# A mixer product in seven 64-row halves per tile instead of eight, in a three-stage block on one Trainium2 core

## The chip, the core and the metric

The kernel runs on one core of a Trainium2 chip. The core has a matrix engine (PE, whose weight loads are listed as PEld), three elementwise engines (DVE, ACT, POOL) and a queue, SP, from which this kernel issues all its DMAs. Time is device time of one execution in microseconds, lower is better. Before the change the median of three runs is 190.23 us (189.8 to 190.86).

## What is computed

The input x has 2048 rows of 448 bf16 numbers. With LN for layer normalisation without weights:

```
h   = x + Attention(LN(x))          16 heads of 28; each row attends to rows i, i-2, ..., i-14
n   = LN(h)
y   = gelu(LN(n) @ w1)              448 -> 448
g0..g3 = four groups of 112 columns of y, moved by +1, -1, +2, -2 rows, zeros moved in
n1  = n + concat(g0, g1, g2, g3) @ w2
out = h + n1 + gelu(LN(n1) @ w3) @ w4       448 -> 1792 -> 448
```

The change concerns `y` (the mixer's first product and its gelu) and the product with `w2` (the mixer's second product).

## The kernel before, in words

Rows are handled in four blocks of 512 rows (t = 0 to 3) up to the mixer's first product, and in five units after it (2, 4, 4, 4 and 2 tiles of 128 rows). The phases of a block are N1 (first normalisation), A1 (queries, keys), V (values), A2 (products of queries and shifted keys), S (softmax), A3 (weighted values), O (output product and residual), B1 (second normalisation) and M (the mixer's first product with its gelu). The phases of a unit are B2 (the mixer's second product), T (third normalisation), W3 (448 -> 1792 with gelu) and B3 (1792 -> 448 and the store). A block or unit number follows the name: M1 is the first product of block 1, B21 the second product of unit 1.

**Matmuls in pairs of halves.** Most products have a contraction of 448, cut into pieces of at most 64 rows. Two pieces run at once, one in the upper and one in the lower 64 rows of the array. `duo` takes two output groups A and B and lists their upper and lower pieces: in a first series A's upper pieces run beside B's lower ones, in a second B's upper beside A's lower. Seven pieces of 64 rows would hold 448 exactly, and the products over normalised rows do it so: their transposed copies overlap by 64 rows, so that one output of a pair takes four upper and three lower pieces and the other three and four (`sums`).

**The mixer's second product** can't do so before the change, because its contraction is split by the row shifts: each group of 112 lies in `gT` in partitions 0 to 111, and is read at its own shift (`SHIFT`). A tile takes an upper piece of 64 and a lower piece of 48 rows from each of four groups, that is eight pieces, and a pair of tiles 16 matmuls of 448 columns. There are eight such pairs of tiles in the kernel (one in B20, two each in B21, B22, B23, one in B24).

**The order of the work** is a table of numbers, `ORDER`: operation k of the recorded program stands at the place that the table gives it, and each engine and the SP queue carry out their operations in the order in which they stand there. Waits are then derived from what each operation reads and writes, and from eight PSUM banks and small pools of buffers that are given out along the table. `OTHER` names operations that run on their second engine: copies out of PSUM that DVE makes instead of ACT, and residual additions that DVE makes instead of POOL. An engine waits at the head of its list, and all behind it waits too.

**ACT's tables.** `gelu` and the `exp`/`ln` of the softmax and of the normalisations need different tables on ACT. Each change from one to the other is an ACT_TABLE_LOAD; there are 12 in the program, before and after.

All instructions of the engines are issued from one line (L1012 before, L1032 after), so the profile's groups are told apart by the names of the tiles: `w_s,arena` are the mixer's second product, `actT,w_s` its first, `arena<-ps 112x512` its gelus, `xin<-ps` the attention's residual, `wo_s,actT` its output product, `qk_r` the products of A2, `bd_r` the spread weights of A3, `h3T<-ps` the gelus of W3, `lntm` normalised rows.

Of the kernel before, what the change touches and what calls it, by code (L numbers as in the profile page):

```python
# [5 lines left out]
ACT = mybir.ActivationFunctionType  # L6
# [13 lines left out]
STAGE = '....'  # L20
ALONE = False
ORDER = """
# [29 lines left out]
"""  # L52
OTHER = """
94 187 189 549 550 551 685 686 755 756 815 816
"""
FULL = (4,)
FILL = (1, 1, 0, 0)
# [228 lines left out]
def bass_sequential_preLN__sliding_local_dilated__mixer_s_mlp__prompt_kernel(  # L286
# [6 lines left out]
    NST = SEQ // 512  # L293
# [11 lines left out]

    SHIFT = (-1, 1, -2, 2)
    GC = D // 4


    A_W3 = 0  # L310
# [9 lines left out]
    with ExitStack() as es:  # L320
        def sb(name, shape, dt):
            return es.enter_context(nc.sbuf_tensor(name, shape, dt))
# [8 lines left out]
        actT = sb("actT", [128, NACT, 4, 4, 128], BF16)  # L331
        h3T = sb("h3T", [128, NF + 2, 512], BF16)
        wo_s = sb("wo_s", [128, 4, D], BF16)
        w1_s = sb("w1_s", [128, 4, D], BF16)
        w2_s = sb("w2_s", [128, 4, D], BF16)
        ident = sb("ident", [128, 128], BF16)
        zc = sb("zc", [128, 4, 2, 32], BF16)
# [115 lines left out]
        wo_v = A_wo.rearrange("(c j k) n -> j k c n", c=4, j=4)  # L453
        for j in range(4):
            dma("wo%d" % j, wo_s[32 * j:32 * j + DH, :, :], wo_v[j], DH * D * 8)
        load_rows("w1", w1_s, B_w1, 0, D)
        dma("w2", w2_s[0:GC, :, :], B_w2.rearrange("(c k) n -> k c n", k=GC), D * D * 2)
        load_rows("w3", w3_s, B_w3, 0, F)
        loads = [op for op in S.ops if op.is_dma]
        for a, b in zip(loads, loads[1:]):  # L460
            b.odeps.add(a)
# [390 lines left out]
        def phase_B1(t):  # L852
            ln = _Tile(P_ln)
            summed = STATS["B1"][t] == "a"
            if summed:
                sums_stats(1, range(4 * t, 4 * t + 4), lambda i: xin[:, i, :], ln)
            else:
                for i in range(4 * t, 4 * t + 4):
                    ln_stats(1, xin[:, i, :], i)
            norms = norms_of("B1", t, 4)  # L860
            rstd(1, 4 * t, 4, summed, norms, POWER["B1"][t])
            for n, i in enumerate(range(4 * t, 4 * t + 4)):
                normalize(1, i, ln, n, xin[:, i, :], TURN["B1"][t], summed, norms[n])
            a = transposed(ln, TURN["B1"][t])
            S.tag = "M%d" % t

            def group(g, upper):
                b = _Tile(P_bank)
                return sums(lambda lo, n: b(halves(lambda v: v[0:GC, lo:lo + n], n // 128)), lambda c, part: w1_s[part, c, g * GC:(g + 1) * GC],
                            lambda c, part, lo, n: rows(a, c, lo // 128, n // 128, part), upper), \  # L870
                    lambda: act(gT[0:GC, g, 2 + t * 512:2 + (t + 1) * 512], b(lambda v: v[0:GC, :]), ACT.Gelu_apprx_tanh)

            for g in (0, 2):
                (A, ev_a), (B, ev_b) = group(g, True), group(g + 1, False)
                duo(A, B, ((0, 512),))
                ev_a()
                ev_b()
# [10 lines left out]
        def phase_B2(u):  # L888
            tiles = UNITS[u]
            summed = STATS["B2"][u] == "a"  # L890

            def group(i):
                b = _Tile(P_bank)

                def side(part):
                    return [(gT[part, c, 2 + i * 128 + SHIFT[c]:130 + i * 128 + SHIFT[c]], (lambda lo, m, c=c: w2_s[part, c, lo:lo + m])) for c in range(4)]

                def out():
                    kw = dict(accum_out=mv[:, 2, i, 0:1]) if summed else {}
                    dve("scalar_tensor_tensor", out=xb[i], in0=xin[:, i, :], scalar=rs_y[:, 1, 0, i:i + 1], in1=b(lambda v: v[:, 0:D]), op0=ALU.mult, op1=ALU.add, **kw)  # L900
                    if not summed:
                        ln_stats(2, xb[i], i)

                return (lambda lo, n: b(lambda v: v[:, lo:lo + n]), side(TOP), side(slice(64, GC))), out

            for i in tiles[::2]:
                (A, out_a), (B, out_b) = group(i), group(i + 1)
                duo(A, B, ((0, D),))
                out_a()
                out_b()  # L910
            ln = _Tile(P_ln)
            if summed:
                sums_stats(2, tiles, lambda i: xb[i], ln)
            S.tag = "T%d" % u
            norms = norms_of("B2", u, len(tiles))
            rstd(2, tiles[0], len(tiles), summed, norms, POWER["B2"][u])
            for n, i in enumerate(tiles):
                normalize(2, i, ln, n, xb[i], TURN["B2"][u], summed, norms[n])
            for i in tiles:
                both = dict(out=xb[i], in0=xb[i], in1=xin[:, i, :], op=ALU.add)  # L920
                S.add("pool", "tensor_tensor", alts=[("dve", [("tensor_tensor", both)])], **both)
            b2_a[u] = transposed(ln, TURN["B2"][u], len(tiles))
# [131 lines left out]
```

## Time and profile before

| | before |
|---|---|
| median of 3 runs | 190.23 us (189.8 to 190.86) |
| the profiled execution | 188.86 us, its span 187.1 us |
| PE busy | 179.9 us, 96% of the span |
| DVE busy | 129.1 us, 69% |
| ACT busy | 124.6 us, 67% |
| POOL busy | 19.8 us, 11% |
| granted TensorE clock | 1.0 |

A row of the chain of waits gives its start, its length and the work; a row of the timeline its start, its length, engine, line, operation, output and inputs, shapes, the count of merged instructions, and in brackets the idle time just ahead and who ended it. A table by stretches gives for each stretch the busy time of each engine with the count of its instructions. A matmul's own duration is its latency; two halves of the array and successive matmuls overlap, so the pace of matmuls is read from the distance of starts.

### The profile page before, as it was taken

Reading aid. Unit: us, or ns where it says so; the run is one execution under the profiler, and the core shown is the slowest. Engines: PE = TensorE matmul, PEld = TensorE weight load, DVE = VectorE, ACT = ScalarE, POOL = GpSimd, SP = SyncE. Lnnn points to the kernel's source line nnn. Section 1 sums busy time; section 2 is a strip of 40 time slices with the busy share of each in tenths; the row PEclk is TensorE's granted clock in tenths of the full one; section 3 lists DMA queues with packets and bytes.
Section 4 is the critical chain, followed back from the end, with each engine's and each line's share of the span. In section 5 each row is a group of like instructions: output and inputs, shape, how many; then the busy total and the mean of one; then the engine's idle time right before and its main releaser. Section 6 shows DMA issues by size and latency. Waiting matters only on the chain.

```text
span 187.1 us, 5625 instructions
## 1 busy us (share of the span) xinstructions
PE 179.9 (96%) x2434; PEld 96.1 (51%) x2434; DVE 129.1 (69%) x233; ACT 124.6 (67%) x286; POOL 19.8 (11%) x50
## 2 busy tenths in 40 slices
PE   6899999989989989999999999999999999999994
PEld 2586434345433555565655455555555444455773
DVE  6899999999999999999797930196871015005222
ACT  3579999999999999999674977910275013830340
POOL 3430000000000002000240000037045000000000
DMA  5924193356307996596543060016005004300012
GB/s 146 346 101 104 12 188 69 77 126 143 105 4 117 213 257 263 88 332 116 126 31 85 5 137 0 4 22 157 10 0 116 0 0 129 77 0 28 0 53 75
DMA packets 36576, 18.05 MB, mean 96 GB/s; under 512 B 25304, under 2 KB 36040, under 8 KB 36552
## 3 DMA queue, kind: packets, MB, share of 16 engines
q1 hardware_dynamic: 36552, 17.70, 39.5%
q8 instruction: 19, 0.31, 0.7%
q14 instruction: 5, 0.04, 0.1%
HBM read 7.91 MB, written 1.84 MB: 52 GB/s over the span
## 4 chain that ended last, share of the span: by engine, by line
PE 78%; DVE 16%; ACT 3%; DMA 1%; issue 1%
PE ps L1012 78%; DVE bd_r L1012 7%; DVE qk_r L1012 4%; DVE lntm L1012 2%; DVE st L1012 1%; DMA xin<-in_A_x_dram 1%; DVE mx L1012 1%; DVE ls L1012 1%; ACT vt L1012 1%; ACT xin L1012 0%; ACT ls L1012 0%; DVE pb L1012 0%; ACT arena L1012 0%; ACT rs_x L1012 0%; ACT rs_y L1012 0%
## 5 line engine op out<-in xcount | busy, mean ns | idle before, releaser
L1012 PE MATMUL ps<-actT,arena 64*128 64x512 bf16 (+1 forms) x756 | 69.6, 329 | 0.2
L1012 ACT ACTIVATE h3T<-ps 128x512 bf16<-128x512 f32 (+1 forms) x70 | 30.9, 518 | 41.1 <-PE ps L1012 40.8
L1012 PEld LDWEIGHTS ps<-actT,arena 64*128 64x128 bf16 x756 | 37.0, 94 | 28.0 <-PE ps L1012 1.9
L1012 PE MATMUL ps<-arena,h3T 64*128 64x448 bf16 (+2 forms) x434 | 45.4, 343 | 0.1
L1012 DVE SCALAR_TENSOR_TENSOR ost<-ps,mrs,arena 128x448 bf16<-128x448 f32 (+1 forms) x17 | 10.7, 653 | 37.4 <-PE ps L1012 33.7
L1012 ACT ACTIVATE arena<-ps 128x512 bf16<-128x512 f32 (+3 forms) x64 | 32.3, 542 | 6.2 <-PE ps L1012 5.8
L1012 PEld LDWEIGHTS ps<-arena,h3T 64*128 64x128 bf16 (+1 forms) x434 | 23.6, 94 | 18.9 <-PE ps L1012 0.5
L1012 DVE TENSOR_TENSOR qk_r<-arena 128x4096 bf16<-128x4096 bf16 (+1 forms) x16 | 32.0, 2014 | 0.1
L1012 POOL TENSOR_TENSOR arena<-arena,xin 128x448 f32<-128x448 f32 x9 | 10.9, 1243 | 96.6 <-DVE lntm L1012 96.6
L1012 DVE TENSOR_TENSOR bd_r<-arena,bmask 80x2048 bf16<-80x2048 bf16 x16 | 18.8, 1215 | 0.2
L1012 DVE TENSOR_SCALAR lntm<-arena,mv,rs_y 128x512 bf16<-128x512 f32 x14 | 7.2, 537 | 13.2 <-ACT rs_y L1012 11.4
L1012 PE MATMUL ps<-wo_s,actT 64*128 64x448 bf16 x128 | 14.5, 350 | 0.8 <-ACT actT L1012 0.6
L1012 PE MATMUL ps<-w_s,arena 64*128 64x448 bf16 (+1 forms) x128 | 14.5, 350 | 0.1
L1012 ACT ACTIVATE actT<-ps 128x512 bf16<-128x512 f32 (+2 forms) x21 | 12.8, 648 | 1.5 <-PE ps L1012 1.5
L1012 PE MATMUL ps<-actT,w_s 64*112 64x512 bf16 x112 | 13.4, 378 | 0.1
L1012 PE MATMUL ps<-arena,actT 64*128 64x448 bf16 x112 | 13.1, 349 | 0.1
L1012 ACT ACTIVATE lntm<-xin,nm 128x448 bf16<-128x448 bf16 x16 | 10.5, 662 | 2.6 <-DVE nm L1012 2.4
L1012 DVE SCALAR_TENSOR_TENSOR arena<-xin,rs_y,ps 128x448 f32<-128x448 bf16 x16 | 10.4, 672 | 0.4 <-PE ps L1012 0.4
L1012 PEld LDWEIGHTS ps<-actT,w_s 64*112 64x112 bf16 x112 | 7.0, 127 | 4.8 <-PE ps L1012 0.5
L1012 DVE BATCH_NORM_STATS2 st<-xin 128x6 f32<-128x448 bf16 x16 | 9.1, 613 | 0.4 <-DMA xin<-in_A_x_dram 0.4
L1012 PEld LDWEIGHTS ps<-wo_s,actT 64*128 64x128 bf16 x128 | 5.5, 94 | 6.8 <-ACT actT L1012 1.5
L1012 PEld LDWEIGHTS ps<-w_s,arena 64*128 64x128 bf16 (+1 forms) x128 | 6.0, 94 | 5.8 <-PE ps L1012 0.5
(69 smaller groups left out, 155.1 us busy)
## 6 DMA issues: line engine op xcount, KB each, us to landing
arena<-in_B_w_dram SPq DMA_DIRECT2D x2, 896.0 KB, 6.4
out_dram<-ost SPq DMA_DIRECT2D x15, 112.0 KB, 2.3
arena<-in_B_w_dram SPq DMA_DIRECT2D x2, 784.0 KB, 6.1
vw<-vt SPq DMA_DIRECT2D x4, 320.0 KB, 3.9
vw<-vt SPq DMA_DIRECT2D x4, 256.0 KB, 4.3
arena<-in_A_wqkv_dram SPq DMA_DIRECT2D x2, 448.0 KB, 4.5
xin<-in_A_x_dram SPq DMA_DIRECT2D x2, 448.0 KB, 5.0
xin<-in_A_x_dram SPq DMA_DIRECT2D x3, 224.0 KB, 5.0
```

The lines of the kernel that those rows point to most:

```text
L1012: inst = getattr(eng, meth)(**kw)
```

## The change

Group 3's 112 columns of `y` are split: 64 of them (336 to 399) stay a group of their own, and the other 48 (400 to 447) are dealt out, 16 to each of the groups 0, 1 and 2, which so become 128 rows high. The first product computes the 16 columns together with a group's own 112 (`w1_s` now holds 128 columns per group, put together by six loads and two copies on POOL), and computes group 3's 64 columns twice, in the upper and the lower half. The 16 rows belong to another shift than the group they ride in. So each of the groups 0 to 2 gets, besides its gelu of 128x512, a second gelu of the 16 rows from the same PSUM bank, written 3, 1 or 4 columns further left, over what the first gelu left there. In the last block three small memsets fill what is moved in. In the second product a tile then takes seven pieces of 64 rows: four upper and three lower for the first tile of a pair, three and four for the second. `w2_s` holds the rows in the same arrangement (four loads instead of one).

```diff
+    GX = 16
-        w1_s = sb("w1_s", [128, 4, D], BF16)
+        w1_s = sb("w1_s", [128, 4, 448 + 112], BF16)
...
-        load_rows("w1", w1_s, B_w1, 0, D)
-        dma("w2", w2_s[0:GC, :, :], B_w2.rearrange("(c k) n -> k c n", k=GC), D * D * 2)
+        for c in range(4):
+            dma("w1%s" % "abcd"[c], w1_s[:, c, 0:384].rearrange("p (g n) -> p g n", g=3)[:, :, GX:],
+                B_w1[64 * (0, 2, 3, 5)[c]:64 * (0, 2, 3, 5)[c] + 128, 0:3 * GC].rearrange("k (g n) -> k g n", g=3), 128 * 3 * GC * 2)
+        load_rows("w1e", w1_s[:, :, 448:448 + GC], B_w1, 3 * GC, GC)
+        dma("w2", w2_s[GX:128, 0:3, :], B_w2[0:3 * GC, :].rearrange("(c k) n -> k c n", k=GC), 3 * GC * D * 2)
+        dma("w2x", w2_s[0:GX, 0:3, :], B_w2[400:, :].rearrange("(c k) n -> k c n", k=GX), 3 * GX * D * 2)
+        for h in range(2):
+            dma("w2%s" % "ab"[h], w2_s[64 * h:64 * h + 64, 3, :], B_w2[3 * GC:400, :], 64 * D * 2)
         load_rows("w3", w3_s, B_w3, 0, F)
+        pool("tensor_copy", out=w1_s[:, :, 0:384].rearrange("p c (g n) -> p c g n", g=3)[:, :, :, 0:GX], in_=w1_s[:, :, 512:].rearrange("p c (g n) -> p c g n", g=3))
+        pool("tensor_copy", out=w1_s[:, :, 384:448], in_=w1_s[:, :, 448:512])
...
-                    lambda: act(gT[0:GC, g, 2 + t * 512:2 + (t + 1) * 512], b(lambda v: v[0:GC, :]), ACT.Gelu_apprx_tanh)
+                def evict():
+                    at = 2 + t * 512
+                    act(gT[:, g, at:at + 512], b(), ACT.Gelu_apprx_tanh)
+                    if g < 3:
+                        at -= SHIFT[3] - SHIFT[g]
+                        skip = max(0, -at)
+                        act(gT[0:GX, g, at + skip:at + 512], b(lambda v: v[0:GX, skip:]), ACT.Gelu_apprx_tanh)
+                        if t == NST - 1:
+                            pool("memset", ap=gT[0:GX, g, at + 512:2 + SEQ], constant=0.0)
...
-                return (lambda lo, n: b(lambda v: v[:, lo:lo + n]), side(TOP), side(slice(64, GC))), out
+                return (lambda lo, n: b(lambda v: v[:, lo:lo + n]), side(TOP, 3 + upper), side(BOT, 4 - upper)), out
...
 ORDER = """
-29 0 1 6 7 33 34 35 5 8 48 9 53 49 39 40 41 42 43 44 45 46 47 30 32 2 50 54 11 10 58 51 52 60 59 55 61 56 62 57 63 65
...
+5 38 39 0 1 48 49 50 51 52 53 54 55 56 42 45 7 6 8 40 57 58 9 62 63 2 59 60 61 11 10 67 69 68 70 64 65 71 72 66 73 96
...
 OTHER = """
-94 187 189 549 550 551 685 686 755 756 815 816
+103 117 195 197 402 516 522 573 574 636 637 638 639 707 778 779 781 840
```

The table of numbers is a new one for the whole program, and three kinds of work changed engine with it: four copies out of PSUM went from ACT to DVE (one in A10, one in A32, two in A33), and two of the residual additions from POOL to DVE. Two places of the order matter to the prediction.

ACT from the end of the softmax of block 2 to the first gelus of W30. `arena<-ps 80x512` are the softmax's last copies, then come the gelus of M0, copies of A32 (`actT<-ps`) and A13 (`arena<-ps 128x512`), the statistics of B20 (`lntm,mv<-arena,nm`), the gelus of M1, and the statistics of block 2 (`lntm,mv<-xin,nm`). Before:

```order
L1012 ACTIVATE arena<-ps 80x512 x2
L1012 ACT_TABLE_LOAD
L1012 ACTIVATE arena<-ps 112x512 x4
L1012 ACTIVATE actT<-ps 128x512 x3
L1012 ACTIVATE arena<-ps 128x512 x2
L1012 ACTIVATE actT<-ps 128x512
L1007 ACT_TABLE_LOAD
L1012 ACTIVATE rs_y<-rs_x 128x4
L1012 ACTIVATE lntm,mv<-arena,nm 128x448 x2
L1012 ACTIVATE rs_x<-mv,epsilon 128x2
L1012 ACTIVATE rs_y<-rs_x 128x2
L1012 ACT_TABLE_LOAD
```

And of the change, from the gelus of M0 (the three rows with 16 partitions and the two of 128x512 around them) on:

```order
L1032 ACTIVATE arena<-ps 16x510
L1032 ACTIVATE actT<-ps 128x512
L1032 ACTIVATE arena<-ps 128x512
L1032 ACTIVATE actT<-ps 128x512
L1032 ACTIVATE arena<-ps 128x512
L1027 ACT_TABLE_LOAD
L1032 ACTIVATE rs_y<-rs_x 128x4
L1032 ACTIVATE lntm,mv<-arena,nm 128x448 x2
L1032 ACTIVATE rs_x<-mv,epsilon 128x2
L1032 ACTIVATE actT<-ps 128x512
L1032 ACTIVATE rs_y<-rs_x 128x2
L1032 ACT_TABLE_LOAD
```

Seven gelus of M0 stand where four stood, four copies instead of six ahead of the table load, and one copy of A32 has moved behind it, between the `ln` and the `exp` of T0; after the last load come seven gelus of M1 instead of four.

PE from the first product of block 0 to the second product of unit 1. `actT,w_s` are M0 and M1, `bd_r,vw` A32, `wo_s,actT` O2, `qk_r,zc` A23, `w_s,arena` B20 and then B21, `actT,arena 128x256` W30. Before:

```order
L1012 MATMUL ps<-actT,w_s 112x512 x28
L1012 MATMUL ps<-bd_r,vw 32x64 x96
L1012 MATMUL ps<-w_s,arena 128x448 x8
L1012 MATMUL ps<-bd_r,vw 32x64 x32
L1012 MATMUL ps<-w_s,arena 128x448 x8
L1012 MATMUL ps<-wo_s,actT 128x448 x8
...
L1012 MATMUL ps<-actT,w_s 112x512 x14
L1012 MATMUL ps<-qk_r,zc 32x32x8x2 x16
L1012 MATMUL ps<-w_s,arena 128x448 x16
L1012 MATMUL ps<-actT,arena 128x256 x28
```

And of the change:

```order
L1032 MATMUL ps<-bd_r,vw 32x64 x96
L1032 MATMUL ps<-w_s,arena 128x448 x14
L1032 MATMUL ps<-actT,w_s 128x512 x16
L1032 MATMUL ps<-wo_s,actT 128x448 x8
L1032 MATMUL ps<-actT,w_s 128x512 x6
L1032 MATMUL ps<-wo_s,actT 128x448 x8
L1032 MATMUL ps<-actT,w_s 128x512 x6
L1032 MATMUL ps<-wo_s,actT 128x448 x16
L1032 MATMUL ps<-qk_r,zc 32x32x8x2 x16
L1032 MATMUL ps<-w_s,arena 128x448 x14
L1032 MATMUL ps<-actT,arena 128x256 x42
```

B20 now stands in one piece behind all of A32, M1 earlier among O2, and of B21's first pair of tiles alone (14 matmuls) the next W30 is the neighbour; its first eight matmuls read two gelus of M1, its last six read M1's three 16-row gelus, which are the last of ACT's seven.

More of the change, by code (lines that the diff above doesn't have):

```diff
@@ L868, in group @@
                 b = _Tile(P_bank)
-                return sums(lambda lo, n: b(halves(lambda v: v[0:GC, lo:lo + n], n // 128)), lambda c, part: w1_s[part, c, g * GC:(g + 1) * GC],
-                            lambda c, part, lo, n: rows(a, c, lo // 128, n // 128, part), upper), \
-                    lambda: act(gT[0:GC, g, 2 + t * 512:2 + (t + 1) * 512], b(lambda v: v[0:GC, :]), ACT.Gelu_apprx_tanh)
+                def evict():
[7 more added lines that the diff above has]
+                            pool("memset", ap=gT[0:GX, g, at + 512:2 + SEQ], constant=0.0)
+                return sums(lambda lo, n: b(halves(lambda v: v[:, lo:lo + n], n // 128)), lambda c, part: w1_s[part, c, g * 128:g * 128 + 128],
+                            lambda c, part, lo, n: rows(a, c, lo // 128, n // 128, part), upper), evict
             for g in (0, 2):
@@ L890, in phase_B2, with group, side @@
             summed = STATS["B2"][u] == "a"
-            def group(i):
+            def group(i, upper):
                 b = _Tile(P_bank)
-                def side(part):
-                    return [(gT[part, c, 2 + i * 128 + SHIFT[c]:130 + i * 128 + SHIFT[c]], (lambda lo, m, c=c: w2_s[part, c, lo:lo + m])) for c in range(4)]
+                def side(part, chunks):
+                    return [(gT[part, c, 2 + i * 128 + SHIFT[c]:130 + i * 128 + SHIFT[c]], (lambda lo, m, c=c: w2_s[part, c, lo:lo + m])) for c in range(chunks)]
                 def out():
@@ L902, in out @@
                         ln_stats(2, xb[i], i)
-                return (lambda lo, n: b(lambda v: v[:, lo:lo + n]), side(TOP), side(slice(64, GC))), out
+                return (lambda lo, n: b(lambda v: v[:, lo:lo + n]), side(TOP, 3 + upper), side(BOT, 4 - upper)), out
             for i in tiles[::2]:
-                (A, out_a), (B, out_b) = group(i), group(i + 1)
+                (A, out_a), (B, out_b) = group(i, True), group(i + 1, False)
                 duo(A, B, ((0, D),))
```

57 rows, old and new, of the table ORDER are left out of this document.

## The prediction

> **What bounds the kernel now.** I read the page's busy times first, then the table by stretches, then the chain of waits.
>
> ```profile
> PE 179.9 (96%) x2434; PEld 96.1 (51%) x2434; DVE 129.1 (69%) x233; ACT 124.6 (67%) x286; POOL 19.8 (11%) x50
> ```
>
> ```profile
> 50.00:66.00 16.00, 14.93 (x306) 6.95 (x294) 15.81 (x27) 15.66 (x39) 0.00 (x0) 1.00 0.55 105
> 66.00:80.00 14.00, 13.52 (x208) 7.05 (x208) 13.89 (x24) 13.48 (x32) 1.31 (x2) 1.00 0.74 203
> 80.00:95.00 15.00, 14.87 (x206) 9.02 (x206) 13.83 (x29) 12.78 (x27) 1.37 (x1) 1.00 0.64 171
> 95.00:110.00 15.00, 15.00 (x264) 7.83 (x266) 12.69 (x32) 11.54 (x25) 2.00 (x2) 1.00 0.38 60
> ```
>
> ```profile
> 62.80 3.41 DVE bd_r L1012 x3
> ...
> 66.35 7.96 PE ps L1012 x134
> ...
> 88.82 95.76 PE ps L1012 x1110
> ```
>
> The average says PE. The stretches (columns PE, PEld, DVE, ACT, POOL) say more: until about 80 us three engines are full at once, DVE 99% and ACT 96% from 66 to 80; only behind 95 us is PE at 100%, with room on the others. The chain runs through DVE up to 66 us, then on PE, from 88.8 us without a break. So a microsecond of matmuls removed behind 89 us is worth a microsecond; ahead of that, work added to ACT or DVE delays what PE waits for. The change takes work from PE and gives more to ACT, nearly half of it between 64 and 80 us.
>
> **The gain.** Between two starts in the timeline, four pairs of halves of the mixer's second product take 0.76 us:
>
> ```profile
> 99.38 0.92 PE L1012 MATMUL ps<-w_s,arena 64*128 64x448 bf16 x8
> 100.14 0.92 PE L1012 MATMUL ps<-wo_s,actT 64*128 64x448 bf16 x8
> 100.89 0.93 PE L1012 MATMUL ps<-w_s,arena 64*128 64x448 bf16 x8
> ```
>
> That is 0.19 us a pair. Each of eight pairs of tiles loses one: 8 x 0.19 = **1.5 us**, of which B20 and B21 (three pairs of tiles) have 0.57 and B22 to B24 0.95.
>
> **The price of a 16-row gelu** is in no row. The nearest on ACT, by rows of partitions:
>
> ```profile
> L1012 ACT ACTIVATE arena<-ps 112x512 bf16<-112x512 f32 x16 | 8.7, 599 | 1.3 <-PE ps L1012 1.2
> L1012 ACT ACTIVATE h3T<-ps 128x256 bf16<-128x256 f32 x28 | 8.5, 391 | 11.9 <-PE ps L1012 11.8
> L1012 ACT ACTIVATE arena<-ps 64x256 bf16<-64x256 f32 x16 | 5.8, 378 | 0.2
> ```
>
> 64 partitions cost what 128 cost (378 against 391 ns); the free size decides. So I take a full one, which back to back adds 0.49 us: (2.06 - 0.60) / 3, from the gelus of M0 below. The low end, time in proportion to partitions, is 0.49 / 4 = 0.12 us; the high end is 0.60, one that drains first. Twelve are 5.9 us (1.4 to 7.2) of ACT.
>
> **Where it lands: M0 and M1.** ACT and DVE from 63 to 77 us, and PE:
>
> ```profile
> 63.17 1.28 ACT L1012 ACT_TABLE_LOAD   x1
> 64.47 2.06 ACT L1012 ACTIVATE arena<-ps 112x512 bf16<-112x512 f32 x4
> 66.40 1.60 ACT L1012 ACTIVATE actT<-ps 128x512 bf16<-128x512 f32 x3
> 68.79 0.67 ACT L1012 ACTIVATE actT<-ps 128x512 bf16<-128x512 f32 x1
> 69.48 1.28 ACT L1007 ACT_TABLE_LOAD   x1
> 70.98 0.67 ACT L1012 ACTIVATE lntm<-arena,nm 128x448 bf16<-128x448 f32 x1
> 72.97 1.28 ACT L1012 ACT_TABLE_LOAD   x1
> 74.27 0.60 ACT L1012 ACTIVATE arena<-ps 112x512 bf16<-112x512 f32 x1
> ```
>
> ```profile
> 70.78 0.17 DVE L1012 TENSOR_SCALAR nm<-mv 128x2 f32<-128x2 f32 x1
> ```
>
> ```profile
> 68.73 0.92 PE L1012 MATMUL ps<-wo_s,actT 64*128 64x448 bf16 x8
> 75.14 1.05 PE L1012 MATMUL ps<-qk_r,zc 128*32 128x512 bf16 x16
> 76.12 1.93 PE L1012 MATMUL ps<-w_s,arena 64*128 64x448 bf16 x16
> 77.89 1.69 PE L1012 MATMUL ps<-actT,arena 64*128 64x256 bf16 x28
> ```
>
> Up to 63 us I carry 0.2 us: a copy of A10 comes to DVE (0.42 us for a bf16 copy of that size, 0.69 for DVE's pass over 512 fp32 numbers, the row of `pb` below), most of it where DVE waited anyway:
>
> ```profile
> 8.18 0.42 DVE L1012 COPY actT<-ps 128x512 bf16<-128x512 bf16 x1 [0.49 <-PE ps L1012]
> 11.74 1.32 DVE L1012 TENSOR_SCALAR lntm<-xin,mv,rs_y 128x448 bf16<-128x448 bf16 x4 [0.45 <-ACT rs_y L1012]
> ```
>
> All times of the changed kernel from here are estimates from these rows. M0's gelus start at 64.47 + 0.2 = 64.67 and end after 6 x 0.49 + 0.60 at 68.2. Four copies (0.48 apart, as from 66.40 to 68.79) end at 70.15, the table load at 71.45. DVE's `nm` moves too: 0.2 before, B20 in one piece behind M0's last gelu 0.4, and `mrs` (0.15) ahead of it, so it ends near 71.55 and the Square starts at 71.65, not 70.98: +0.67. The copy of A32 moved in behind adds 0.5: the load starts at 74.14, **M1's first gelu at 75.44 instead of 74.27**. Its fourth ends at 77.5, its seventh at 79.0.
>
> PE gets to B21 earlier than that: B20 from 68.25 (1.33 us), M1's 28 matmuls (3.04), O2's 32 (3.05, by the distances above), A23's 16 (0.98), so 76.6. There its first eight matmuls wait 0.9 us for M1's fourth gelu, the last six 0.7 for the seventh, and it is through at 79.6; before, at 77.89. Queued behind are W30, the rest of A23 and B21; W30 could not fill the gap, since its rows are turned by a DMA that leaves after T0, itself later by about 1.3 us. **PE is 1.7 us later with 0.38 us less to do.**
>
> **From there to 102 us.**
>
> ```profile
> 79.31 0.93 ACT L1012 ACTIVATE h3T<-ps 128x256 bf16<-128x256 f32 x3
> ```
>
> ```profile
> 89.02 0.69 DVE L1012 TENSOR_TENSOR pb<-ls,mx 128x512 bf16<-128x512 f32 x1
> ```
>
> ```profile
> 90.45 3.21 PE L1012 MATMUL ps<-actT,w_s 64*112 64x512 bf16 x28
> 93.50 1.49 PE L1012 MATMUL ps<-arena,h3T 64*128 64x448 bf16 x14
> ```
>
> On ACT, M1's end at 79.0 is followed by four Squares (2.6), six gelus (0.27 each: (0.93 - 0.39) / 2), two table loads around the softmax's exp (which waits for DVE until 84.6), and W30's last eight gelus, 87.1 to 89.4. B30's second fourteen matmuls need the last of them, so B30's 42 end at 92.1. DVE has by then gained a copy (0.6), `mrs` (0.15) and T1's first row, which waits for POOL and now stands ahead of `pb`, and lost one addition (0.6): `pb` ends at 92.1, before at 89.7. The softmax's transposes so run at 92.1 instead of 90.2. M2 and A33 follow with 3.05 us and four DVE spreads of 1.15 with a copy between; O3's last matmul ends at 102.25, where before, with 0.76 us of B22 ahead of it, it ended at 100.89. At equal work: **+2.1 us**. The three 16-row gelus of M3 are covered: from 95 to 110 us ACT already has 3.5 of 15 us free, and PE has W31 to run meanwhile.
>
> **The sum.** From 102 us PE ran without a break before and, with more pieces ready, should now; there 0.95 us of the gain remains. +2.1 - 0.95 = **+1.2 us**. The profiled execution would go from 188.86 to 190.0; that one is 1.37 us under the median of the runs shown, so I add the difference to the median: 190.23 + 1.2 = **191.4 us**. With gelus at the low end M1's seventh ends 1.3 us earlier, at 77.7 (three times 0.12 behind the fourth, which the moved copy and DVE still hold to 77.3), and the sum is about -0.1; at the high end six gelus of 0.60 add 6 x 0.11 = 0.7 and three copies 0.3, and it is +2.2. Where the new order removes a stall that the rows of before hold, it can be lower than either.
>
> **What I cost at nothing.** Seven more loads (0.55 us each on SP) stand ahead of the transposes of B10 and B11. SP had this wait ahead of B10's:
>
> ```profile
> 47.01 1.10 SPq L1012 DMA_DIRECT2D w_s<-in_B_w_dram  x2
> 56.41 2.97 SPq L1012 DMA_TRANSPOSE actT<-lntm  x1
> 59.42 2.02 SPq L1012 DMA_DIRECT2D vw<-vt  x3
> ```
>
> Four more of `w1` and the three `vw` that moved ahead take 4.2 of the 8.3 idle us; the three more of `w2` take the place of the `vw`. If that cover fails M0 is late by what is over. The two copies and three memsets on POOL lie in its idle time (11% busy).
>
> The first product's weights go from 112 to 128 columns, and loads of 112 take longer here:
>
> ```profile
> L1012 PEld LDWEIGHTS ps<-actT,w_s 64*112 64x112 bf16 x112 | 7.0, 127 | 4.8 <-PE ps L1012 0.5 <-ACT h3T L1012 0.3
> L1012 PEld LDWEIGHTS ps<-w_s,arena 64*128 64x128 bf16 x64 | 5.6, 94 | 5.8 <-PE ps L1012 0.5 <-ACT arena L1012 0.4 <-ACT h3T L1012 0.2
> ```
>
> ```profile
> 145.82 1.04 PE L1012 MATMUL ps<-actT,arena 64*128 64x512 bf16 x8
> 146.69 2.81 PE L1012 MATMUL ps<-arena,h3T 64*128 64x448 bf16 x28
> ```
>
> If loads lay on the path, M would gain 112 x 33 ns = 3.7 us. But M2's 14 pairs take 3.05 us, 0.218 a pair, and pairs of 512 columns whose weights have 128 columns take the same (four in 0.87 us): the loads lie under the matmuls, and I take nothing. [...]
>
> **The rivals.** *Hidden gelus, faster*: the new order keeps PE fed at B21 and S3, the 5.9 us on ACT cost at most 0.5, and 1.5 - 0.5 = 1.0 comes off: 189.2. For it: after 95 us ACT has room, and the whole table is new, so stalls that I did not look for (PE idles 1.1 us from 50 to 66) may be gone. Against: ACT was full just where six of the twelve come. 0.22. *No change*: the delay of M1 is half of mine, since PE is later at B21 too, and gain and loss cancel: 190.4. 0.28. *SP, slower still*: the loads of 224-byte rows take twice the time of those shown, 4 us more, B10's transposes and M0 start 1 us late, and DVE's chain follows: 192.4. It decides once the loads ahead exceed 8.3 us. 0.08. *The weight loads count*: a quarter of the 3.7 us comes off too, beside 1.5 with the gelus hidden: 187.8; the pace of M2 speaks against it. 0.02.
>
> [...]
>
> **How the numbers follow.** My forecast has 0.40, its own range 190.8 to 192.0. A measurement of this kernel tells 0.5% (0.95 us) from no change: faster 0.22 + 0.02 = 0.24, same 0.28 and a little of the forecast's lower edge, 0.32, slower 0.44. For 8 in 10 the range goes from 189.1 to 192.6.
>
> **What would show it.** Right: M1's first gelu over 1 us later against M0's first matmul; PE idle ahead of B21's matmuls, ended by ACT, 1 to 2 us in all; S3's transposes near 92; PE unbroken behind 102. Wrong: 16-row gelus clearly under 0.4 us; B21 without a wait; M0's matmuls waiting for a DMA; or PE's work as a whole not 1.5 us less.

## The result, and the profile after

The change takes **191.26 us** (median of 10 runs, 190.59 to 191.85) against 190.21 us before (10 runs beside it): ratio **1.0058, 95% interval 1.004 to 1.0077**, 1.1 us slower. The profiled execution after has 191.85 us, the longest of its ten, and a span of 189.8 us; the one before lay 1.35 us under its median. The two traces so differ by 2.7 us, the medians by 1.1, and stages are compared below from a common mark, M0's first matmul (61.87 us before, 63.52 after). Ratios are taken over fast executions alone (one of six in runs 5 and 7 was slow), so a ratio can differ from the quotient of the medians beside it.

Busy times of the page, and the same four stretches as before (columns PE, PEld, DVE, ACT, POOL, then granted clock, DMA share, GB/s):

```profile
PE 179.5 (95%) x2418; PEld 92.3 (49%) x2418; DVE 132.6 (70%) x239; ACT 129.0 (68%) x294; POOL 18.7 (10%) x53
```

```profile
50.00:66.00 16.00, 14.60 (x282) 5.87 (x282) 15.78 (x29) 15.26 (x38) 2.22 (x2) 1.00 0.49 99
66.00:80.00 14.00, 12.98 (x240) 5.68 (x239) 13.68 (x26) 13.76 (x29) 2.02 (x2) 1.00 0.84 213
80.00:95.00 15.00, 14.31 (x198) 8.32 (x200) 13.81 (x28) 13.02 (x33) 1.03 (x1) 1.00 0.61 166
95.00:110.00 15.00, 15.00 (x266) 7.44 (x264) 14.27 (x28) 12.63 (x26) 0.00 (x0) 1.00 0.24 53
```

From 66 to 80 us DVE and ACT are both at 98%, and PE has fallen from 13.52 to 12.98 us; from 80 to 95 from 14.87 to 14.31. Behind 95 us PE is full again. The chain of waits (start, length, what):

```profile
40.77 3.46 DMA arena<-arena
44.26 2.29 DVE qk_r L1032
...
68.23 1.55 ACT arena L1032 x3
...
71.70 1.29 DVE arena L1032 x4
72.99 0.07 DVE mrs L1032
73.06 0.13 DVE nm L1032
73.19 0.59 DVE actT L1032
73.78 2.20 DVE qk_r L1032
...
81.65 0.68 DVE arena L1032
...
82.38 2.91 PE ps L1032 x40
...
92.46 94.08 PE ps L1032 x1093
```

Before, PE carried the chain from 66.35 us on. Now DVE carries it from 71.70 to 82.3 us, with `mrs` and the copy of A32 (`actT`) on it; just ahead of that stretch the last three gelus of M0 (the row at 68.23) hold B20. The 16-row gelus stand behind others on ACT; the third row, of the groups by form, gives the count, the busy time and the mean ns:

```profile
66.10 3.67 ACT L1032 ACTIVATE arena<-ps 128x512 bf16<-128x512 f32 x7
...
76.86 3.45 ACT L1032 ACTIVATE arena<-ps 128x512 bf16<-128x512 f32 x7
```

```profile
L1032 ACT ACTIVATE arena<-ps 16x512 bf16<-16x512 f32 x10 | 5.4, 573 | 0.0
```

And PE around the places that the prediction names:

```profile
69.92 1.74 PE L1032 MATMUL ps<-w_s,arena 64*128 64x448 bf16 x14 [0.20 <-ACT arena L1032]
...
78.97 0.93 PE L1032 MATMUL ps<-w_s,arena 64*128 64x448 bf16 x8
80.36 0.74 PE L1032 MATMUL ps<-w_s,arena 64*128 64x448 bf16 x6 [0.46 <-ACT arena L1032]
80.94 2.70 PE L1032 MATMUL ps<-actT,arena 64*128 64x256 bf16 x42
...
93.79 0.46 PE L1032 MATMUL ps<-ident,pb 64*80 64x64 bf16 x16
```

From M0's first matmul, W30 starts at 17.42 us (80.94 - 63.52), 1.40 later than before, and S3's transposes at 30.27, 1.98 later. Behind S3 the change is faster: from there to the end of B34's matmuls it takes 93.4 us, before 94.4.

### The profile page after: what moved, and what is told of

Read it like the earlier page. It is cut to its first block, busy times and chain, and to the rows that moved or that the text cites. A ratio compares the mean times of both kernels' runs of the same rounds, so it can differ in the third digit from the quotient of the medians.

```text
span 189.8 us, 5616 instructions
## 1 busy us (share of the span) xinstructions
PE 179.5 (95%) x2418; PEld 92.3 (49%) x2418; DVE 132.6 (70%) x239; ACT 129.0 (68%) x294; POOL 18.7 (10%) x53
## 4 chain that ended last, share of the span: by engine, by line
PE 60%; DVE 21%; ACT 8%; DMA 5%; issue 2%; SPq 2%; DVEq 0%
PE ps L1032 60%; DVE qk_r L1032 10%; ACT arena L1032 3%; DMA arena<-in_A_wqkv_dram 3%; DVE bd_r L1032 3%; DVE lntm L1032 3%; ACT vt L1032 2%; DMA arena<-arena 2%; SPq L1032 2%; DVE xin L1032 1%; DVE arena L1032 1%; ACT actT L1032 1%; DVE mx L1032 1%; DVE ls L1032 1%; DVE ost L1032 1%
## 5 line engine op out<-in xcount | busy, mean ns | idle before, releaser
L1032 ACT ACTIVATE h3T<-ps 128x512 bf16<-128x512 f32 (+1 forms) x70 | 30.4, 520 | 39.4 <-PE ps L1032 39.2
L1032 PEld LDWEIGHTS ps<-actT,arena 64*128 64x128 bf16 x756 | 35.9, 94 | 30.4 <-PE ps L1032 2.2
L1032 PE MATMUL ps<-arena,h3T 64*128 64x448 bf16 (+2 forms) x434 | 44.7, 343 | 0.1
L1032 ACT ACTIVATE arena<-ps 128x512 bf16<-128x512 f32 (+4 forms) x75 | 37.5, 545 | 5.9 <-PE ps L1032 5.2
L1032 PE MATMUL ps<-actT,w_s 64*128 64x512 bf16 x112 | 13.8, 377 | 0.1
L1032 PE MATMUL ps<-w_s,arena 64*128 64x448 bf16 x112 | 12.9, 350 | 0.8 <-ACT arena L1032 0.7
L1032 POOL TENSOR_TENSOR arena<-arena,xin 128x448 f32<-128x448 f32 x7 | 8.0, 1156 | 54.8 <-DVE lntm L1032 35.6
L1032 ACT ACTIVATE actT<-ps 128x512 bf16<-128x512 f32 (+2 forms) x18 | 10.9, 637 | 0.9 <-PE ps L1032 0.8
L1032 PE MATMUL ps<-qk_r,zc 128*32 128x512 bf16 x112 | 8.4, 383 | 0.6 <-DVE qk_r L1032 0.6
L1032 PEld LDWEIGHTS ps<-w_s,arena 64*128 64x128 bf16 x112 | 5.1, 95 | 7.4 <-ACT arena L1032 1.4
```

What stands on the lines that cost most here:

```text
L1032: inst = getattr(eng, meth)(**kw)
```

## The experiments

Each ratio is to the kernel before on the same chip, beside it; its median there was 189.8 to 190.0 us.

**1. The change without its 16-row gelus.**

```diff
-                        act(gT[0:GX, g, at + skip:at + 512], b(lambda v: v[0:GX, skip:]), ACT.Gelu_apprx_tanh)
```

> The changed kernel without its twelve 16-row gelus (so the 16 rows stay at the wrong shift), nothing else moved. Theory A (as predicted: these gelus on a full ACT cost about 2 us up to 102 us, the seven pieces give 1.5 back): 189.3 to 189.8 us, M1's gelus four in a row, B21 without a wait for ACT. Theory B (the new order itself lost time ahead of M0, the gelus are mostly hidden): 190.8 to 191.2 us.

Measured: 190.84 us, ratio **1.0035 [1.0016, 1.0054]**. Theory A, the forecast's own reading, falls: the twelve gelus cost only 0.0058 - 0.0035 = 0.0023, 0.4 us (with both intervals -0.1 to 0.9), in the change's order. The time lies in theory B's range. PE at B21 and W30 shows where the price of M1's gelus went:

```profile
78.03 1.74 PE L1030 MATMUL ps<-w_s,arena 64*128 64x448 bf16 x14
...
81.44 1.26 PE L1030 MATMUL ps<-actT,arena 64*128 64x256 bf16 x20 [0.47 <-DVE arena L1030]
```

B21's 14 matmuls run without the wait of 0.46 us for ACT, and W30 then waits 0.47 us for DVE, for a bank that B21's own eviction holds. The wait was not removed, it changed its owner. What the gelus do cost is there before: B20 starts 5.92 us behind M0's first matmul in this run, 6.40 in the change, where M0's last gelus hold it. From M0's first matmul to S3's transposes this run takes 29.81 us, the change 30.27 and the kernel before 28.29; so 0.46 us are the gelus', and 1.5 us remain without them, behind M0 and not ahead of it as theory B had it.

**2. Eight pieces in the change's order**: the program of before, with the change's table from which the added operations are taken out.

> The kernel before (eight pieces, no 16-row gelu, old loads) in the new order of the work, the added operations left out of the table. Theory A: the gelus' 2 us go and the 1.5 us of matmuls come back, 190.6 to 190.9 us. Theory B (the order loses 2.5 us, the change of the product gains 1.5): 192.5 to 192.8 us.

Measured: 191.61 us, ratio **1.0074 [1.0046, 1.0102]**, between the two theories. The order alone costs 1.4 us (0.9 to 1.9) on a program that has nothing to hide. The seven pieces in it give 0.0074 - 0.0035 = 0.0039, 0.7 us (0.1 to 1.4). By the traces this gain lies behind S3, where this run takes 94.4 us to the end of B34's matmuls, as the kernel before, and run 1 takes 93.4, as the change.

**3. One transfer moved forward on SP.** `kkc1` (operation 252), which A22's products wait for, goes from six places further back to directly behind its sister:

```diff
-20 251 461 ... 472 252 382
+20 251 252 461 ... 472 382
```

> The changed kernel with one DMA moved forward on SP: the 16 columns of keys that block 2 takes over from block 1, which in the profile landed when DVE had waited 0.7 us for them ahead of A22. Theory A: DVE sets the pace there, so 0.5 to 0.8 us come off, 190.5 to 190.8 us. Theory B (the wait is made up later, at the softmax of block 2, where ACT and DVE wait for each other): 191.1 to 191.4 us.

Measured: 190.82 us, ratio **1.0034 [1.0019, 1.0048]**, 0.0024 or 0.45 us less than the change (0 to 0.9), near theory A. SP's rows, of the change and of this run:

```profile
32.23 1.90 SPq L1032 DMA_DIRECT2D arena<-arena  x1
...
40.77 2.11 SPq L1032 DMA_DIRECT2D arena<-arena  x1
```

```profile
31.50 2.34 SPq L1032 DMA_DIRECT2D arena<-arena  x2
```

In the change the second transfer is issued at 40.77 us, behind two that wait for ACT and two loads of `wo`; it is the DMA row at the head of the chain above. Moved, it goes out with the first, and A22's first product on DVE starts at 42.95 us instead of 44.26.

**4. The 16 rows by POOL copies** from SBUF, instead of second gelus:

```diff
-                        act(gT[0:GX, g, at + skip:at + 512], b(lambda v: v[0:GX, skip:]), ACT.Gelu_apprx_tanh)
+                        pool("tensor_copy", out=gT[0:GX, g, at + skip:at + 512], in_=gT[0:GX, g, 2 + t * 512 + skip:2 + (t + 1) * 512])
```

T0's two additions on POOL are moved behind M1's copies.

> The changed kernel with the twelve second gelus replaced by copies on POOL, in place, of the 16 rows to their own shift (the two additions of T0 on POOL behind M1's copies); the outputs stay the same. Theory A: ACT gets 5.9 us back and POOL has room, so most of the 2 us go: 189.5 to 190.3 us. Theory B (POOL's copies end later than ACT's gelus did, or ACT was no limit): 191.1 to 191.6 us.

Measured: 200.85 us, ratio **1.0573 [1.0538, 1.0608]**; no theory had this. POOL, PE and the stretches of this run:

```profile
65.74 5.64 POOL L1032 COPY arena<-arena 16x512 bf16<-16x512 bf16 x2 [9.18 <-ACT arena L1032]
71.33 0.39 POOL L1032 COPY w_s<-w_s 128x256 bf16<-128x256 bf16 x1
```

```profile
71.78 3.42 PE L1032 MATMUL ps<-actT,w_s 64*128 64x512 bf16 x14 [6.54 <-POOL w_s L1032]
```

```profile
68.00:72.00 4.00, 0.22 (x2) 0.13 (x4) 2.35 (x2) 0.00 (x0) 3.73 (x3) 0.50 0.98 364
72.00:76.00 4.00, 3.93 (x82) 1.45 (x82) 0.00 (x0) 0.76 (x2) 0.10 (x1) 0.50 0.57 161
```

Two things were overlooked. The second copy of `w1` stands on POOL behind M0's first shifted copies in the change's table, so M0's last 14 matmuls waited 6.54 us. And of the two 16x512 copies one lasted 5.1 us, where the median of the fourteen POOL copies into `arena` is 0.61. The last two rows show a third thing: with PE busy for 0.22 us of the four from 68 to 72 us the granted clock was 0.50, and it was 0.50 still in the four after, in which PE was busy for 3.93. As a way to do without the gelus this was not tried fairly.

**5 and 6. The order of before, with and without the gelus.** Every operation that both kernels have stands where it stood before; each 16-row gelu stands behind the main gelu of its group, the added loads behind those they replace:

```diff
+... 24 25 26 27 28 29 36 37 199 ...
+... 464 30 31 32 33 563 ...
+... 208 209 204 205 202 203 ...
```

> The whole change (seven pieces, twelve 16-row gelus, the loads and copies for them), but in the order of before: every operation that both kernels have stands where it stood before, on the engine that had it before; each 16-row gelu stands directly behind the main gelu of its group, the added loads behind those they replace. Theory O (the new order itself costs about 1.4 us, whatever it carries; the gelus are nearly hidden): the ratio is about 1.0058 - 0.0074 = 0.998, so 189.4 to 190.4 us. Theory G (the gelus are what costs, and the new order is the cheaper way of taking them in): M0 and M1 are each held by their three gelus, 2 x 1.4 us on ACT where it is full, with little of the 1.5 us of matmuls left to set against it: 191.3 us or more, slower than the change.

> The same as the run in the order of before, with the twelve 16-row gelus left out (so the rows that they should write hold something else, and the shifted sums of the mixer are not the reference's). This is the seven pieces alone in the order of before. By the forecast's own pricing 1.5 us come off, if PE sets the pace in all of B20 to B24: 188.7 us. If only what lies behind 102 us counts (0.95 us, of which eight pieces against seven in the new order showed 0.75): 189.2 to 189.5 us. Theory O and theory G agree here; the difference to the run with the gelus is what the gelus cost in the order of before: 0.4 us by O, 2 us or more by G.

Measured: with the gelus 194.97 us, ratio **1.0221 [1.017, 1.0272]**; without them 189.53 us, **0.9987 [0.9959, 1.0015]**. Theory G holds: in the order of before the same twelve gelus cost 1.0221 - 0.9987 = 0.0234, 4.4 us (3.3 to 5.6). PE's waits there:

```profile
68.50 0.93 PE L1032 MATMUL ps<-w_s,arena 64*128 64x448 bf16 x8 [1.63 <-ACT arena L1032]
...
80.25 0.74 PE L1032 MATMUL ps<-w_s,arena 64*128 64x448 bf16 x6 [1.67 <-ACT arena L1032]
...
121.43 1.50 PE L1032 MATMUL ps<-arena,h3T 64*128 64x448 bf16 x14 [0.44 <-ACT arena L1032]
...
123.48 2.26 PE L1032 MATMUL ps<-w_s,arena 64*128 64x448 bf16 x22 [0.56 <-ACT arena L1032]
```

All four end with a gelu: at B20, at B21, and twice behind M3. The run without gelus hardly gained from its seven pieces, and its PE and SP rows say why:

```profile
67.92 0.93 PE L1030 MATMUL ps<-w_s,arena 64*128 64x448 bf16 x8 [0.81 <-DMA w_s<-in_B_w_dram]
...
71.03 1.04 PE L1030 MATMUL ps<-actT,w_s 64*128 64x512 bf16 x8 [0.39 <-DMA actT<-lntm]
```

```profile
62.09 3.17 SPq L1030 DMA_DIRECT2D w_s<-in_B_w_dram  x4
65.31 2.57 SPq L1030 DMA_TRANSPOSE actT<-lntm  x1
```

Where one load of `w2` stood on SP between B10's and B11's transposes, four stand now; the transposes that M1 needs go out at 65.31 us, 2.5 later than before.

**7 and 8. The same two with `w2`'s loads ahead of B10's transposes**, in SP's idle time:

```diff
-... 24 25 26 27 28 29 36 37 199 ... 464 30 31 32 33 563
+... 24 25 26 27 28 29 30 31 32 33 36 37 199 ... 464 563
```

> The whole change in the order of before, as in the run of that order (ratio 1.0221), but with the four loads of w2 issued directly behind those of w1, in SP's idle time ahead of B10's transposes, instead of between B10's and B11's, where in that run's trace they held B11's transposes up (issued 64.70 instead of 62.83). Theory G (the gelus are what costs in the order of before): there PE waits for gelus at B20 (1.63 us), B21 (1.67) and M3 (1.0), and M1's matmuls came behind those waits anyway, so little changes: ratio 1.018 to 1.022, 193.4 to 194.2 us. Theory L (the loads in SP's queue are what costs there): 1.5 us or more come off, 192 us or less.

> The same without the twelve 16-row gelus (their rows hold something else, so the mixer's sums are not the reference's): the seven pieces alone in the order of before, with w2's loads out of the way. Without gelus the trace of the order of before showed PE waiting 0.81 us at B20 for a load of w2 and 0.39 at M1 for B11's transposes. Theory L: these waits ate the gain of the seven pieces there (ratio 0.9987); without them it shows: 188.4 to 189.2 us, ratio 0.992 to 0.996. If the seven pieces give little in themselves, it stays at 0.997 to 0.999.

Measured: with the gelus 194.6 us, **1.0211 [1.0178, 1.0243]**; without them 188.51 us, **0.9934 [0.9911, 0.9957]**. Both theories hold, each for its own run: the loads ate 0.0053, 1.0 us (0.3 to 1.7), of the gain where no gelus were in the way, and next to nothing where PE waited for gelus anyway. The seven pieces alone are worth 1.25 us, the gelus in this order 0.0277, 5.3 us (4.5 to 6.0). Part of that is the clock (from M0's first matmul to W30's the trace of run 7 takes 20.56 us, that of run 5 at full clock 18.97), by two stretches of the run with gelus:

```profile
66.00:70.00 4.00, 2.20 (x108) 1.29 (x97) 3.73 (x3) 3.94 (x9) 0.00 (x0) 0.99 0.95 263
70.00:72.00 2.00, 2.00 (x14) 0.79 (x12) 1.15 (x3) 1.98 (x4) 0.00 (x0) 0.50 1.03 414
```

Behind the pause at B20 PE was full but at half clock. The trace of run 5 has nearly the same pause (1.63 us, here 1.54) and a clock of 1.00 throughout; it is one of two executions near 193.0 us, while the other four, with a mean clock of 0.98 to 0.99, lie at 195.0 to 196.4.

**9 and 10. Four second series pulled apart**, alone and with run 3's move:

```diff
-622 623 590 598 591 594 595 599
+622 590 623 598 591 594 599 595
-412 413 571 ... 497
+412 571 ... 497 413
-614 325 331 327 615 34 35 ... 577 494 578
+614 325 331 327 34 35 ... 577 494 578 615
```

> The change, with four second series of pairs that stood directly behind their first series moved one place apart: O2's and B21's last, and in W30, so that another series runs between the two. In the trace of the change such a second series starts 0.24 us later than another would. Theory S (these waits of PE for itself are part of what the new order costs, since PE sets the pace from 82 us on): two of the four lie behind 82 us, 0.48 us come off, up to 1.0 with the two ahead of it: 190.3 to 190.8 us. Theory D (ACT's and DVE's chain to the softmax's last product sets the pace there, and PE has slack): 191.1 to 191.4 us, as the change.

> The four series pulled apart, and the transfer for A22 issued directly behind its sister, as in the run of that transfer alone (ratio 1.0034). By theory S the two gains add, and it is 189.9 to 190.4 us; by theory D the transfer alone counts: 190.7 to 190.9 us.

Measured: 192.29 us, **1.0116 [1.0082, 1.0149]**, and 191.51 us, **1.0083 [1.0051, 1.0116]**: slower than the change by 0.006, and by 0.005 against run 3. Theory S falls. The trace of run 9 has these rows in A23 and W30:

```profile
76.84 0.61 PE L1032 MATMUL ps<-qk_r,zc 128*32 128x512 bf16 x8 [0.65 <-ACT arena L1032]
...
82.59 1.27 PE L1032 MATMUL ps<-actT,arena 64*128 64x256 bf16 x20 [1.06 <-DVE arena L1032]
```

DVE empties B21's and O2's tiles, and I had moved their last matmuls back; and A23, moved ahead of O2's last series, now waits for one of M1's gelus. What PE gained it lost in waits for DVE and ACT. Neither run shows how much slack PE had in the change's own order.

**11 and 12. The order of before up to M0's first matmul, the change's from there; then the same with PE kept busy.** Run 12 adds to run 11 eight matmuls that nobody reads:

```diff
+        S.tag = "fill"
+        f = _Tile(P_bank)
+        mms([(f(), ident[:], w1_s[:, 0, 0:512], k == 0, k == 7, 512, None) for k in range(8)])
```

> The change, with the order of before (and w2's loads ahead of B10's transposes) up to M0's first matmul, and the order of the change for all that is left. Theory F (the part of the new order's cost that lies ahead of M0 is a loss that nothing pays back: the transfer for A22 behind four others on SP, 0.45 us by its own run, and a copy and a row more on DVE, some 0.5): 0.9 to 1.1 us come off, 190.2 to 190.4 us, ratio 1.000 to 1.002. Theory T (the copies that the new order puts on DVE early make room on ACT that M0 and M1 need, so the front can't be had back alone): 191.0 us or more.

> The run with the order of before up to M0 (ratio 1.0209), with eight matmuls of 512 columns added on PE between M0's third series and A32's first product, into a bank that nobody reads: they fill the 1.81 us for which PE stood still there (64.72 to 66.53 us in that run's trace), and nothing waits for them but PE's own next matmul. In that trace the granted clock goes to 0.50 at 68.2 us, just behind this pause, and is back at full only at about 75.5. Theory C (the pause costs the clock, and half the clock over 7 us is the 3.5 us by which that run missed its expectation): with PE busy the clock stays at 1.0, and it is 190.0 to 190.8 us, ratio 1.000 to 1.005. Theory N (the loss is in the spliced order itself: DVE and ACT are later by what the front no longer does, and PE's clock only follows from its having less to do): 193.3 us or more, ratio 1.018 to 1.022.

Measured: run 11 193.9 us, **1.0209 [1.0189, 1.023]**; run 12, with more work, 192.14 us, **1.0113 [1.0093, 1.0132]**. PE and two stretches of run 11, then of run 12:

```profile
66.53 0.42 PE L1032 MATMUL ps<-bd_r,vw 80*32 80x64 bf16 x32 [1.81 <-DVE nm L1032]
...
69.34 3.05 PE L1032 MATMUL ps<-w_s,arena 64*128 64x448 bf16 x14 [0.42 <-ACT arena L1032]
```

```profile
64.00:68.00 4.00, 2.19 (x93) 1.01 (x92) 3.44 (x5) 2.81 (x6) 0.00 (x0) 1.00 1.02 175
68.00:72.00 4.00, 3.51 (x86) 1.57 (x73) 2.45 (x2) 3.98 (x8) 0.00 (x0) 0.52 0.99 357
```

```profile
69.71 1.74 PE L1035 MATMUL ps<-w_s,arena 64*128 64x448 bf16 x14 [0.62 <-ACT arena L1035]
```

```profile
64.00:68.00 4.00, 3.76 (x53) 1.45 (x52) 3.44 (x5) 2.85 (x5) 0.00 (x0) 1.00 1.08 186
68.00:72.00 4.00, 3.31 (x120) 1.85 (x120) 3.33 (x3) 3.87 (x8) 0.00 (x0) 1.00 0.92 340
```

With the pause filled the clock stays at 1.00, B20's 14 matmuls take 1.74 us instead of 3.05, and 0.0096, 1.8 us (1.3 to 2.4), come back; the mean clock is 0.98 in all four executions of run 11 and 1.0 in all six of run 12. Theory C's mechanism is shown, its size was too large. Theory F falls, and the rest of the miss bears theory T out in that the front can't be had back alone, though by a place in PE's order that waits for DVE and not by ACT's copies. Run 12's chain has

```profile
66.90 1.19 PE ps L1035 x38
...
68.11 1.55 ACT arena L1035 x3
```

M0's last series stands behind A32's first product, which DVE lets go at 66.53 us in run 11 and which starts at 66.90 here; that series' gelus end at 69.66, and B20 starts at 69.71, hardly before the change's 69.92, though M0 had started 1.25 us earlier. Here an early front gained nothing, since the order behind it is cut for a late one.

None of these kernels beats the one before while it computes the whole; the nearest is run 3, at 1.0034.

## Why the prediction was right, and where it was not

**The sum was right, and in part by luck.** Its steps from M0's first matmul on came nearly as forecast; what they were put down to did not. Differences between the ratios of the runs, in us:

| | order of before (runs 7, 8) | order of the change (runs 1, 2 and the change) |
|---|---|---|
| seven pieces instead of eight | -1.25 | -0.7 |
| twelve 16-row gelus | +5.3 | +0.4 |
| the order itself | 0 | +1.4 with eight pieces |

In the change, +1.4 - 0.7 + 0.4 = 1.1 us, which is the measured difference by construction. Forecast were +2.1 of delay and -0.95 of gain, the same sum split otherwise: 1.3 us of it hung on the gelus, which cost 0.4, and the sum with gelus at the low end was put at -0.1, where +0.7 was measured without any. The two errors nearly cancel, and that is luck.

So is the last step from traces to medians. Between the two traces the stretches add up to 2.6 us (1.65 up to M0, 1.98 to S3, -1.0 behind it); the medians differ by 1.1, since the one trace was short for its kernel and the other long. The forecast's 0.2 for the front was too small, and its sum met the medians all the same.

- *The gain.* 1.5 us of matmuls, 0.95 of them left behind 102 us. Right: from S3 to the end the change takes 1.0 us less, and the seven pieces alone 1.25 us [0.8, 1.7]. Of what lies ahead of 102 us the change's order kept nothing, as said. PE's busy time fell by 0.4 us only, and a fall of less than 1.5 was named as a sign of being wrong; the 16 matmuls are gone, but five more series (see the last section) start late behind their first, which adds 1.1 (an estimate, 5 x 0.22).
- *The price of a gelu.* Right: six steps of M0's seven take 3.67 - 0.57 = 3.10, 0.52 us each, M1's 0.48, against 0.49; and 16 partitions cost what 128 cost, 573 ns against 596 for the 128x512 rows into the same tile, copies among them.
- *M1's first gelu.* Right in size: 13.34 us behind M0's first matmul, before 12.40, so +0.94; forecast 1.17 less the 0.2 of the front, though the sign of being right was put at over 1. Half of it is the order's: without the gelus (run 1) it is 12.86, +0.46.
- *PE at B21 and W30.* The delay was right, +1.40 (forecast 1.5 from M0), the waits were not: one of 0.46 us instead of 0.9 and 0.7. PE reached B21 at 15.45 us behind M0's first matmul, not at 14.5, since B20 began 0.2 later and the matmuls from there on took 9.05 us (69.92 to 78.97) instead of 8.4, so it had less to wait for. Of the idle time ahead of B21 that was named as a sign, 1 to 2 us, 0.46 came.
- *S3.* Right: +1.98 from M0 on, forecast 1.7; `pb` and T1's first row stand on DVE as read:

```profile
91.97 0.55 DVE L1032 TENSOR_SCALAR lntm<-arena,mv,rs_y 128x512 bf16<-128x512 f32 x1 [0.56 <-POOL rs_y L1032]
92.64 0.69 DVE L1032 TENSOR_TENSOR pb<-ls,mx 128x512 bf16<-128x512 f32 x1
```

- *Behind 102 us* PE ran unbroken, from 92.46 on. M3's gelus are covered: the change spreads M3 over 116.2 to 122.1 us, with B3's matmuls between; in the order of before they held PE for 0.44 and 0.56 us.
- *Weight loads* of the first product got shorter, 94 ns with 128 columns against 127 with 112, and the matmuls did not, as said: M0's 28 take 3.19 us in run 5 and 3.21 before.

**The step that failed is the one on what the sum hangs on**: "With gelus at the low end ... the sum is about -0.1". With gelus at nothing (run 1) it was +0.7. I had priced each delay at ACT and then added DVE's copy, `mrs` and T1's row as if they were the gelus' company. They bind by themselves: with the copy of A32 and `mrs` on its list DVE carries the chain from 71.7 to 82.3 us in the change and from 70.7 to 81.3 in run 2, which has no such gelu (in run 1 the chain goes through ACT's list from 72.3 to 78.0 in between, DVE being busy all the same). The gelus add 0.4 us in all twelve, and by the traces at B20. No run takes the copy or `mrs` back alone, so how the 1.4 us of the order are shared among its moves stays open. Priced apart, the gelus are 5.3 us in the old order, and the change's order is the cheaper way of taking them in, paid at 1.4 us.

**Two sizes were missed.** The front was put at +0.2 us; one transfer on SP alone is 0.45, and M0 starts at 62.5 to 63.5 us in the five traces with the change's whole front, at 61.9 to 62.3 in the seven with the old one. I had looked on SP for loads ahead of the transposes, and not at a transfer that the table moves back behind a waiting one. The rival "hidden gelus" was half right: they are hidden, at 0.4 us where it allowed 0.5, and what hides them costs more than the seven pieces gain. The SP rival had its mechanism in the wrong kernel: four loads ahead of B11's transposes cost 1.0 us in run 6; in the change SP stands idle from 62.98 to 64.67 us ahead of these transposes, until DVE has their rows ready (64.64).

**Open**: why the other executions of the kernel before are some 1.3 us longer than the profiled one; how much of the first 0.7 us of the change's trace, a late landing of a `wqkv` load, is its order; whether the 16 rows can be had by small transfers, which was not tried.

## What to carry to other kernels

A change that comes with a new order has two prices, and the order's is to be read like any other: go through the list of every engine that was near full for what it now has to do earlier, and through SP's for what stands behind a waiting entry. To see whether an addition is cheap, put it into the old order as well; here the same gelus cost 5.3 us there and 0.4 here, and the difference was paid elsewhere. Where three engines are nearly full, a wait on PE that one engine's work causes can come back under another's name when it is removed, as in runs 1 and 9.

## What the runs showed of the hardware

**In two runs the granted clock fell to 0.50 behind a pause of PE of less than 2 us.** In run 11 PE stood still for 1.81 us at once and was busy for 2.19 us of the four from 64 to 68; the granted clock then was 0.52 and 0.63 over the next two stretches of 4 us. In run 7 the pause was 1.54 us, and the clock 0.50 from 70 to 72 us. In run 5 one of 1.63 us left the clock at 1.00. Filling the pause of run 11 with work for nobody gave 1.8 us back. The half clock lasted about 3.4 us in run 7, 6.8 in run 11 and 10.2 in run 4, where PE had stood still for 6.54 us (estimates from the granted clock in stretches of 2 us: 0.99, 0.50 and 0.66 from 68 us on in run 7, 0.54, 0.50, 0.50 and 0.76 from 68 on in run 11, 0.95, five times 0.50 and 0.99 from 66 on in run 4). How much PE was busy just ahead does not tell the cases apart: of the four us from 66 to 70 it was for 2.20 in run 7, whose clock fell, and for 2.05 in run 5, whose clock did not. What decides it was not shown.

**One POOL copy took 5.1 us beside four rows of DVE.** In run 4 it began at 65.74 us and ended at 70.83, 0.48 us behind these, which left DVE no gap:

```profile
64.67 3.49 DVE L1032 TENSOR_TENSOR bd_r<-arena,bmask 80x2048 bf16<-80x2048 bf16 x3
68.07 2.28 DVE L1032 TENSOR_TENSOR qk_r<-arena 128x4096 bf16<-128x4096 bf16 x1
```

The median of the fourteen POOL copies into `arena` is 0.61 us. That POOL stood still until DVE's four rows were through is the author's estimate from these times; no run moves the copy away from them.

**A second series directly behind its first** starts about 0.22 us later than another would (414 ns behind the last start, where the pace of 448 columns is 190); in both traces PE is idle for 0.06 us just ahead of it, and what ends that is PE's own result (`<-PE ps`); the change's order has 14 such places and the one before 9. Pulling four apart gained nothing, since waits for DVE and ACT took their place.
